# Banded attention as PE blocks with a mask matmul, a two-step scan, and an issue order made by a list scheduler, in place of attention by elementwise products and a four-step chunk scan

## The chip, the cores and the metric

The kernel runs on one core of a Trainium2 chip. Times are device microseconds of one execution. A kernel's time is the median of its runs, and the profile comes from one of those executions; its span is about 2 us shorter than the time of the same run. PE is the matmul engine, PEld its weight load (it overlaps PE), DVE the vector engine, ACT the scalar engine, POOL the GpSimd engine, SP the sync engine that issues most transfers; a "q" behind a name (PEq, SPq) means the engine's instruction sequencer or its transfer queue. PSUM is the memory that matmuls write to; to evict a PSUM tile is to copy it out, after which the tile can be used again.

A run counts as slow when it is over 1.5% above the fastest run of the same kernel. Comparisons use fast runs; where a median over all runs is given, it is called that or all runs were fast.

## The reference, cut to what matters

Two independent halves, concatenated on the last axis. Everything is bf16 in and out; S = 2048, D = 448, 16 heads of 28.

```python
def A(x, wqkv, wo):                      # attention over 8 positions: t, t-2, ..., t-14
    q, k, v = split_heads(x @ wqkv)      # H=16, Dh=28
    idx = pos[:, None] - arange(8)[None] * 2
    logits = einsum("bhsd,bhswd->bhsw", q, k[idx]) * Dh ** -0.5   # masked where idx < 0
    o = einsum("bhsw,bhswd->bhsd", softmax(logits), v[idx])
    return merge_heads(o) @ wo

def B(x, Lambda, Bm, C, log_dt, Dskip):  # complex state of 448, a recurrence over 2048 steps
    dt = exp(log_dt);  Lam_bar = exp(dt * Lambda)
    Bu = x @ (((Lam_bar - 1) / Lambda)[:, None] * Bm).T
    h[t] = Lam_bar * h[t-1] + Bu[t]
    return 2 * real(h @ C.T) + x * Dskip
out = concatenate([A, B], axis=-1)
```

Offsets step by two, so even positions attend to even ones only and odd to odd ones. The change uses that.

## The kernel before

The parts that the change replaces. All of it is straight-line code: the order of the instructions on each engine is the order of the text.

```python
# projections: 192 matmuls, each group of 4 evicted by ACT
def proj(t, dst, joff):
    for j in range(J):
        ps = psum.tile([128, 512], F32, tag="mm")
        for kt in range(4):
            PE.matmul(ps[:, 0:D], xTA[:, kt, j, :], wq[:, kt, t * D:(t + 1) * D], ...)      # L144
        ACT.copy(o_ap, ps[:, 0:D].rearrange("p (h d) -> p d h", h=H))
        next_group()                     # transposes on PE, in between
# ... (halo copies by DMA, parameters, tables)

def ssm_chunk_scan(hf):                  # scan over chunks of T = 4 steps
    # rotate by cos/sin tables ...
    V.tensor_tensor_scan(sc[:, ri, i, :], rT[...], vv[:, ri, i, :], 0.0, ALU.mult, ALU.add)   # L278
    # rotate back ...
# then 72 repair matmuls for the three inner steps (L294-L296), each group evicted by ACT

# attention logits: elementwise products on DVE, then a tree of adds
for g in range(4):
    for wi in range(2):
        V.tensor_tensor(pr..., q_s[:], k_s[:, off:off + J]..., ALU.mult)                      # L327
        V.tensor_tensor(pr[:, 0:14, :], pr[:, 0:14, :], pr[:, 14:28, :], ALU.add)             # L329
        ...
# ... softmax on DVE and ACT
for jg in range(J // JG):
    for w in range(W):
        V.tensor_tensor(pv[:], attn[...].to_broadcast(...), v_s[:, off:off + JG], ALU.mult)   # L380
        for jj in range(JG):
            for kt in range(4):          # an identity matmul that sums over the 8 offsets
                PE.matmul(acc[0:KT, kt, jj, :], pvf[:, jj, KT * kt:KT * (kt + 1)], ident[:], ...)  # L385
    ACT.copy(oT[...], acc[0:KT])
    # ... output projection of the group before
```

Of the kernel before, what the change touches and what calls it, by code (L numbers as in the profile page):

```python
# [9 lines left out]
F32 = mybir.dt.float32  # L10
ALU = mybir.AluOpType
ACTF = mybir.ActivationFunctionType

S, D, H, DH, W = 2048, 448, 16, 28, 8
J = 16
HALO = 14
JK = J + HALO
JH = J * H
KT = 112
T = 4  # L20
NC = S // T
PI = math.pi
SHR = 1.0 - 1e-6
MAGIC = 12582912.0


@with_exitstack
def kernel(
# [17 lines left out]
    V = nc.vector  # L46
    ACT = nc.scalar
    PE = nc.tensor

    const = ctx.enter_context(tc.tile_pool(name="const", bufs=1))  # L50
    psum = ctx.enter_context(tc.tile_pool(name="ps", bufs=4, space=bass.MemoryType.PSUM))
    pst_ctx = ExitStack()
    psum_t = pst_ctx.enter_context(tc.tile_pool(name="pst", bufs=2, space=bass.MemoryType.PSUM))
    ident = const.tile([128, 128], BF16, tag="ident")
    make_identity(nc, ident[:])

    bk = ctx.enter_context(tc.tile_pool(name="b_keep", bufs=1, side="right"))
    bx = ctx.enter_context(tc.tile_pool(name="b_x", bufs=1, side="right"))
    bn_ctx = ExitStack()
    bn = bn_ctx.enter_context(tc.tile_pool(name="b_n", bufs=1, side="right"))  # L60
    ak = ctx.enter_context(tc.tile_pool(name="a_keep", bufs=1))
    qk_ctx = ExitStack()
    qkp = qk_ctx.enter_context(tc.tile_pool(name="a_qk", bufs=1))
    ain_ctx = ExitStack()
    ain = ain_ctx.enter_context(tc.tile_pool(name="a_in", bufs=1))

    def rows112(src):
        return src.rearrange("(k p) n -> p k n", p=KT)
    xnA = ain.tile([128, J, D], BF16, tag="xnA")
    xA_r = A_x[0].rearrange("(p j) d -> p j d", j=J)  # L70
    nc.sync.dma_start(xnA[:, 0:4, :], xA_r[:, 0:4, :])
    nc.sync.dma_start(xnA[:, 4:8, :], xA_r[:, 4:8, :])
    nc.sync.dma_start(xnA[:, 8:12, :], xA_r[:, 8:12, :])
    nc.sync.dma_start(xnA[:, 12:16, :], xA_r[:, 12:16, :])
    wq = ain.tile([KT, 4, 3 * D], BF16, tag="wqkv")
    nc.sync.dma_start(wq[:, 0:2], rows112(A_wqkv)[:, 0:2])
    nc.sync.dma_start(wq[:, 2:4], rows112(A_wqkv)[:, 2:4])

    raws = []
    for i, (vec, name) in enumerate(((B_Lambda_re, "lre"), (B_Lambda_im, "lim"), (B_log_dt, "ld"), (B_Dskip, "dsk"))):  # L80
        raw = const.tile([KT, 4], BF16, tag=name + "_raw", name=name + "_raw")
        nc.sync.dma_start(raw[:], vec.rearrange("(t i) -> i t", i=KT))
        raws.append(raw)
    Cn = bn.tile([KT, 2, 4, D], BF16, tag="Cn")
    nc.sync.dma_start(Cn[:, 0], rows112(B_C_re))
    nc.gpsimd.dma_start(Cn[:, 1], rows112(B_C_im))
    Bn = bn.tile([KT, 2, 4, D], BF16, tag="Bn")
    nc.sync.dma_start(Bn[:, 0], rows112(B_B_re))
    nc.gpsimd.dma_start(Bn[:, 1], rows112(B_B_im))
    xnB = bx.tile([128, 4, T, D], BF16, tag="xnB")  # L90
    xB_r = B_x[0].rearrange("(cb p j) d -> p cb j d", p=128, j=T)
    nc.sync.dma_start(xnB[:, 0:2], xB_r[:, 0:2])
    nc.gpsimd.dma_start(xnB[:, 2:4], xB_r[:, 2:4])

    xTA = ain.tile([KT, 4, J, 128], BF16, tag="xTA")
    CT = bn.tile([KT, 4, 2, D], BF16, tag="CT")
    BT = bk.tile([KT, 4, 2 * D], BF16, tag="BT")
    xT4 = bk.tile([KT, 4, T, NC], BF16, tag="xT4")
    idk = ident[0:KT, 0:KT]

    def g_xta(jg, kt):
        tp = psum_t.tile([128, 4, 128], BF16, tag="tp", name="tp")
        for jj in range(4):
            PE.transpose(tp[0:KT, jj, :], xnA[:, 4 * jg + jj, KT * kt:KT * (kt + 1)], ident[:])  # L104
        V.tensor_copy(xTA[:, kt, 4 * jg:4 * jg + 4, :], tp[0:KT])  # L105

    def g_bt(ri, kt):
        tp = psum_t.tile([128, 4, 128], BF16, tag="tp", name="tp")
        for pt in range(4):
            PE.transpose(tp[0:KT, pt, 0:KT], Bn[:, ri, pt, KT * kt:KT * (kt + 1)], idk)  # L110
        ACT.copy(BT[:, kt, ri * D:(ri + 1) * D].rearrange("p (a b) -> p a b", a=4), tp[0:KT, :, 0:KT])

    def g_x4(kt, j):
        tp = psum_t.tile([128, 4, 128], BF16, tag="tp", name="tp")
        for cb in range(4):
            PE.transpose(tp[0:KT, cb, :], xnB[:, cb, j, KT * kt:KT * (kt + 1)], ident[:])  # L116
        ACT.copy(xT4[:, kt, j, :], tp[0:KT])

    def g_ct(ri, pt):
        tp = psum_t.tile([128, 4, 128], BF16, tag="tp", name="tp")  # L120
        for dtile in range(4):
            PE.transpose(tp[0:KT, dtile, 0:KT], Cn[:, ri, dtile, KT * pt:KT * (pt + 1)], idk)
        V.tensor_copy(CT[:, pt, ri, :].rearrange("p (a b) -> p a b", a=4), tp[0:KT, :, 0:KT])

    groups = ([(g_xta, (jg, kt)) for jg in range(4) for kt in range(4)]
              + [(g_ct, (ri, pt)) for ri in range(2) for pt in range(4)]
              + [(g_bt, (ri, kt)) for ri in range(2) for kt in range(4)]
              + [(g_x4, (kt, j)) for j in range(T) for kt in range(4)])

    def next_group(n=1, late=False):  # L130
        for _ in range(n):
            if groups and (late or groups[0][0] in (g_xta, g_ct)):
                fn, args = groups.pop(0)
                fn(*args)
    next_group(4)

    q_s = qkp.tile([128, DH, J, H], BF16, tag="q_s")
    k_s = qkp.tile([128, JK, DH, H], BF16, tag="k_s")
    v_s = ak.tile([128, JK, DH, H], BF16, tag="v_s")
    def proj(t, dst, joff):  # L140
        for j in range(J):
            ps = psum.tile([128, 512], F32, tag="mm")
            for kt in range(4):
                PE.matmul(ps[:, 0:D], xTA[:, kt, j, :], wq[:, kt, t * D:(t + 1) * D], start=(kt == 0), stop=(kt == 3))  # L144
            o_ap = dst[:, :, j, :] if t == 0 else dst[:, joff + j, :, :]
            ACT.copy(o_ap, ps[:, 0:D].rearrange("p (h d) -> p d h", h=H))  # L146
            next_group()
        if t != 0:
            nc.sync.dma_start(dst[1:65, 0:HALO], dst[0:64, J:JK])
            nc.sync.dma_start(dst[65:113, 0:HALO], dst[64:112, J:JK])  # L150
            nc.sync.dma_start(dst[112:128, 0:HALO], dst[111:127, J:JK])
            nc.sync.dma_start(dst[0:1, 0:HALO], dst[0:1, J:JK])

    proj(2, v_s, HALO)
    def pt_(name):
        return const.tile([KT, 4], F32, tag=name, name=name)
    lre, lim, ld, dsk = [pt_(n) for n in ("lre", "lim", "ld", "dsk")]
    for f_, r_ in zip((lre, lim, ld, dsk), raws):
        V.tensor_copy(f_[:], r_[:])
    hpib = const.tile([KT, 1], F32, tag="hpib")  # L160
    nc.gpsimd.memset(hpib[:], 0.5 * PI * SHR)

    def tt(o, a_, b_, op):
        V.tensor_tensor(o[:], a_[:], b_[:], op)
        return o

    def ts(o, a_, s1, op):
        V.tensor_scalar(o[:], a_[:], s1, None, op)
        return o

    def sincos(sin_out, cos_out, y, kM, pool, shape, tagp):
        nfr = pool.tile(shape, F32, tag=tagp + "nfr", name=tagp + "nfr")
        V.scalar_tensor_tensor(nfr[:], kM, -MAGIC, y, ALU.add, ALU.subtract)
        ACT.activation(sin_out, nfr[:], ACTF.Sin, scale=-2 * PI * SHR)
        afr = pool.tile(shape, F32, tag=tagp + "afr", name=tagp + "afr")
        ACT.activation(afr[:], nfr[:], ACTF.Abs)
        ACT.activation(cos_out, afr[:], ACTF.Sin, bias=hpib[:], scale=-2 * PI * SHR)

    dt = pt_("dt"); ACT.activation(dt[:], ld[:], ACTF.Exp)
    are = tt(pt_("are"), dt, lre, ALU.mult)  # L180
    th = tt(pt_("th"), dt, lim, ALU.mult)
    r = pt_("r"); ACT.activation(r[:], are[:], ACTF.Exp)
    rT = pt_("rT"); ACT.activation(rT[:], are[:], ACTF.Exp, scale=float(T))
    f = ts(pt_("f"), th, 1.0 / (2 * PI), ALU.mult)
    fT = ts(pt_("fT"), th, float(T) / (2 * PI), ALU.mult)
    kM1 = pt_("kM1"); V.tensor_scalar(kM1[:], f[:], 1.0, MAGIC, ALU.mult, ALU.add)
    sn = pt_("sn"); cs = pt_("cs")
    sincos(sn[:], cs[:], f[:], kM1[:], const, [KT, 4], "p_")
    pwall = const.tile([KT, T - 1, 3, 4], F32, tag="pwall")
# [58 lines left out]
    for hf, j in [(hf, j) for hf in range(2) for j in range(T)]:  # L248
        if hf == 0 and j < T - 1:
            next_group(4, late=True)  # L250
# [170 lines left out]
```

## Time and profile before

| | before |
|---|---|
| time, median of 3 runs | 229.51 us (227.4 to 229.69) |
| span of the profiled run | 227.3 us |
| busiest engines | PE 80%, DVE 71% |

The page of the kernel before, parts 1 and 2: busy time with share of the span and number of instructions; then three rows of busy tenths in 40 equal slices of the span (9 is 90% or more), and the row of the clock that PE was granted, in tenths of full speed.

```profile
PE 181.1 (80%) x1400; PEld 118.0 (52%) x1400; DVE 161.9 (71%) x200; ACT 105.1 (46%) x186; POOL 4.8 (2%) x18
...
PE   2008995989997999999969400599999996999993
...
DVE  1103779794007999179999999999867999999022
...
PEclk9999999799999799999999955599999999999999
```

Counting slices from 0, 5.7 us each: PE has one hole in slices 22 to 25 (near 127 to 145 us), with a halved clock in it, and one at the start. The chain that ended last, by engine:

```profile
PE 57%; DVE 25%; ACT 8%; DMA 7%; SPq 1%; issue 1%
```

Busy time by stretch; the columns are the stretch, its length, then busy us and number of instructions of PE, PEld, DVE, ACT and POOL, then the granted PE clock, the busy share of the DMA engines, and GB/s.

```profile
20.00:60.00 40.00, 36.33 (x230) 21.24 (x229) 28.16 (x91) 28.91 (x60) 0.00 (x0) 0.96 0.40 89
60.00:95.00 35.00, 33.43 (x214) 21.06 (x212) 21.92 (x11) 25.37 (x48) 0.11 (x1) 0.95 0.20 36
...
120.00:160.00 40.00, 22.75 (x112) 12.69 (x110) 39.86 (x27) 15.15 (x27) 0.37 (x2) 0.79 0.02 6
160.00:195.00 35.00, 33.05 (x367) 24.18 (x366) 30.74 (x30) 11.71 (x16) 0.47 (x2) 1.00 0.19 59
```

PE is the busier engine from 20 to 95 us and from 160 us on, at 90 to 96% of each stretch. From 120 to 160 us DVE works without a pause and PE 57% of the time. Three of the groups that the change removes, with busy us, mean ns of one, and the idle time just before them:

```profile
L327 DVE TENSOR_TENSOR pr<-q_s,k_s 128x7168 bf16<-128x7168 bf16 x8 | 31.1, 3885 | 15.9 <-ACT q_s L146 15.9
...
L380 DVE TENSOR_TENSOR pv<-attn,v_s 128x1792 bf16<-128x1792 bf16 x32 | 32.2, 1082 | 0.0
L385 PE MATMUL acc<-ident,pv 128*112 128x128 bf16 x512 | 29.2, 219 | 2.0 <-ACT oT L387 2.0
```

### The profile page before, as it was taken

Reading aid. Unit: us, or ns where it says so; the run is one execution under the profiler, and the core shown is the slowest. Engines: PE = TensorE matmul, PEld = TensorE weight load, DVE = VectorE, ACT = ScalarE, POOL = GpSimd, SP = SyncE. Lnnn points to the kernel's source line nnn. Section 1 sums busy time; section 2 is a strip of 40 time slices with the busy share of each in tenths; the row PEclk is TensorE's granted clock in tenths of the full one; section 3 lists DMA queues with packets and bytes.
Section 4 is the critical chain, followed back from the end, with each engine's and each line's share of the span. In section 5 each row is a group of like instructions: output and inputs, shape, how many; then the busy total and the mean of one; then the engine's idle time right before and its main releaser. Section 6 shows DMA issues by size and latency. Waiting matters only on the chain.

```text
span 227.3 us, 3441 instructions
## 1 busy us (share of the span) xinstructions
PE 181.1 (80%) x1400; PEld 118.0 (52%) x1400; DVE 161.9 (71%) x200; ACT 105.1 (46%) x186; POOL 4.8 (2%) x18
## 2 busy tenths in 40 slices
PE   2008995989997999999969400599999996999993
PEld 2004662645555666566536200255555696887961
DVE  1103779794007999179999999999867999999022
ACT  2001691898678876454438300293345213234151
POOL 6000000000000000000000000000000000000000
PEclk9999999799999799999999955599999999999999
DMA  6999300392752000000000000001112230020213
GB/s 227 283 291 204 136 4 0 71 178 40 141 108 35 3 0 0 3 0 0 0 0 0 3 0 0 0 0 40 62 43 81 62 114 3 0 84 3 82 36 128
DMA packets 9996, 14.02 MB, mean 62 GB/s; under 512 B 2716, under 2 KB 8188, under 8 KB 9724
## 3 DMA queue, kind: packets, MB, share of 16 engines
q1 hardware_dynamic: 9612, 12.07, 21.2%
q0 software_dynamic: 368, 1.72, 2.6%
q8 instruction: 11, 0.18, 0.3%
q14 instruction: 5, 0.04, 0.1%
HBM read 6.88 MB, written 3.67 MB: 46 GB/s over the span
## 4 chain that ended last, share of the span: by engine, by line
PE 57%; DVE 25%; ACT 8%; DMA 7%; SPq 1%; issue 1%
PE acc L385 13%; PE ps L144 12%; PE ps L306 11%; DMA wq<-in_A_wqkv_dram 7%; PE psf L256 6%; PE ps L367 5%; DVE pr L327 5%; DVE scr L278 4%; DVE pr L329 3%; DVE dg L212 2%; PE tp L116 2%; PE psf L295 2%; PE psf L296 1%; PE ps L308 1%; PE psf L261 1%; PE psf L260 1%
## 5 line engine op out<-in xcount | busy, mean ns | idle before, releaser
L144 PE MATMUL ps<-wq,xTA 112*128 112x448 bf16 x192 | 44.9, 376 | 15.6 <-DMA wq<-in_A_wqkv_dram 11.9
L327 DVE TENSOR_TENSOR pr<-q_s,k_s 128x7168 bf16<-128x7168 bf16 x8 | 31.1, 3885 | 15.9 <-ACT q_s L146 15.9
L256 PE MATMUL psf<-xT_115,BT 112*112 112x512 bf16 x128 | 33.7, 386 | 0.0
L380 DVE TENSOR_TENSOR pv<-attn,v_s 128x1792 bf16<-128x1792 bf16 x32 | 32.2, 1082 | 0.0
L385 PE MATMUL acc<-ident,pv 128*112 128x128 bf16 x512 | 29.2, 219 | 2.0 <-ACT oT L387 2.0
L385 PEld LDWEIGHTS <-pv 128*112 128x112 bf16 x512 | 29.0, 130 | 2.3 <-issue 2.0
L144 PEld LDWEIGHTS <-xTA 112*128 112x128 bf16 x192 | 18.9, 103 | 20.3 <-issue 4.3
L306 PE MATMUL ps<-Cw,Z 112*128 112x448 bf16 x128 | 26.8, 352 | 0.0
L262 ACT CAST Z<-psf 112x512 bf16<-112x512 f32 x32 | 18.8, 587 | 16.9 <-PE psf L261 15.5
L295 PE MATMUL psf<-Z,dg 112*112 112x511 bf16 x24 | 10.1, 419 | 18.8 <-DVE Z L282 18.8
L297 ACT CAST Z<-psf 112x512 bf16<-112x512 f32 x24 | 14.0, 585 | 22.9 <-PE psf L296 21.7
L256 PEld LDWEIGHTS <-BT 112*112 112x112 bf16 x128 | 16.7, 132 | 9.9
L146 ACT CAST v_s<-ps 128x448 bf16<-128x448 f32 x16 | 8.3, 538 | 26.8 <-PE ps L144 26.7
L105 DVE COPY xTA<-tp 112x512 bf16<-112x512 bf16 x16 | 6.7, 422 | 19.6 <-PE tp L104 19.4
L387 ACT CAST oT<-acc 112x2048 bf16<-112x2048 f32 x4 | 7.5, 1865 | 22.8 <-PE acc L385 22.8
L310 ACT CAST yo<-ps 128x448 bf16<-128x448 f32 x16 | 8.3, 531 | 17.9 <-DMA out_dram<-yo 9.8
L104 PEld LDWEIGHTS <-xnA 128*112 128x112 bf16 x64 | 7.3, 164 | 18.0 <-issue 12.5
L306 PEld LDWEIGHTS <-Z 112*128 112x128 bf16 x128 | 11.8, 98 | 9.0
L329 DVE TENSOR_TENSOR pr<-pr 128x3584 bf16<-128x3584 bf16 x8 | 16.1, 2016 | 0.1
L296 PEld LDWEIGHTS <-dg 112*112 112x112 bf16 x24 | 3.4, 142 | 21.5 <-issue 19.9
L367 PE MATMUL ps<-wo_p,oT 112*128 112x448 bf16 x64 | 12.6, 352 | 0.0
L104 PE MATMUL tp<-ident,xnA 128*112 128x128 bf16 x64 | 7.7, 259 | 4.4 <-DMA xnA<-in_A_x_dram 4.3
(131 smaller groups left out, 234.3 us busy)
## 6 DMA issues: line engine op xcount, KB each, us to landing
xnA<-in_A_x_dram SPq DMA_DIRECT2D x4, 448.0 KB, 6.8
out_dram<-yo SPq DMA_DIRECT2D x16, 112.0 KB, 1.7
out_dram<-ya SPq DMA_DIRECT2D x16, 112.0 KB, 1.7
wq<-in_A_wqkv_dram SPq DMA_DIRECT2D x2, 588.0 KB
xnB<-in_B_x_dram POOLq DMA_DIRECT2D x1, 896.0 KB, 13.2
xnB<-in_B_x_dram SPq DMA_DIRECT2D x1, 896.0 KB
v_s<-v_s SPq DMA_DIRECT2D x1, 784.0 KB
k_s<-k_s SPq DMA_DIRECT2D x1, 784.0 KB
```

Of the source, the lines that this page charges most:

```text
L104: PE.transpose(tp[0:KT, jj, :], xnA[:, 4 * jg + jj, KT * kt:KT * (kt + 1)], ident[:])
L144: PE.matmul(ps[:, 0:D], xTA[:, kt, j, :], wq[:, kt, t * D:(t + 1) * D], start=(kt == 0), stop=(kt == 3))
L256: PE.matmul(ps[:], BT[:, kt, ri * D + KT * pt: ri * D + KT * (pt + 1)], xT4[:, kt, j, :], start=(kt == 0), stop=(kt == 3 and j == 0))
L262: ACT.copy(Z[:, ri * 4 + pt, j, :], ps[:])
L295: PE.matmul(ps[:, 1:NC], dg[:, pt, j, ia, :], Z[:, pt, T - 1, 0:NC - 1], start=False, stop=False)
L297: ACT.copy(Z[:, ri * 4 + pt, j, :], ps[:])
L306: PE.matmul(ps[:, 0:D], Z[:, k8, j, cols], Cw[:, k8, :], start=(k8 == 0), stop=False)
L327: V.tensor_tensor(pr.rearrange("p d (j h) -> p d j h", h=H), q_s[:], k_s[:, off:off + J].rearrange("p j d h -> p d j h"), ALU.mult)
L329: V.tensor_tensor(pr[:, 0:14, :], pr[:, 0:14, :], pr[:, 14:28, :], ALU.add)
L367: PE.matmul(ps[:, 0:D], oT[:, kt, j, :], wo_p[:, kt, :], start=(kt == 0), stop=(kt == 3))
L380: V.tensor_tensor(pv[:], attn[:, w, JG * H * jg:JG * H * (jg + 1)].rearrange("p (j h) -> p j h", h=H) .unsqueeze(2).to_broadcast((128, JG, ...
L385: PE.matmul(acc[0:KT, kt, jj, :], pvf[:, jj, KT * kt:KT * (kt + 1)], ident[:], start=(w == 0 and jj == 0), stop=(w == W - 1 and jj == JG - 1))
```

## The change

The intent: give the attention to PE as small blocks, so that DVE has only the normalising left; halve the work of the state space half by a two-step scan, which runs over the first and then the second half of the positions (the half-scans); let the transfers transpose (the prediction calls such a transfer a crossbar load); and interleave the two halves so that PE never runs dry. The diff replaces nearly the whole body. Its core, cut:

```diff
+# attention: per block of 112 or 128 queries of one parity, 4 mask matmuls and 16 score
+# matmuls in four row groups of 32 (28 used), one exponential, 16 matmuls with V,
+# whose 29th column is ones and gives the sum
+            s4 = h["s4"] = pss.tile([128, 4, 512], F32, tag="s4", name="s4")
+            for g in range(4):
+                PE.matmul(s4[:, g, 0:4 * n]..., msk[32 * g:32 * g + 32, 0, :],
+                          msk[32 * g:32 * g + 32, 1:2, c0:c0 + n].to_broadcast((32, 4, n)), start=True, ...)  # L569
+            for s in range(4):
+                for g in range(4):
+                    PE.matmul(s4[:, g, s * n:s * n + n], Kt[32 * g:32 * g + DH, s, par, k0(b):k0(b) + 128],
+                              Qt[32 * g:32 * g + DH, s, par, q0(b):q0(b) + n], ...)                          # L573
+            ACT.activation(P[...], h["s4"][...], ACTF.Exp, scale=SCALE)                                     # L578
+            for hd in range(H):
+                PE.matmul(av[:, 29 * hd:29 * hd + 29], h["P"][:, hd // 4, hd % 4, :], Vt[:, par, b, hd, :], ...)  # L584
+            V.reciprocal(rc, avv[0:n, :, 28])                                                               # L592
+            V.tensor_tensor(O[...], avv[0:n, :, 0:DH], rc.unsqueeze(2).to_broadcast((n, H, DH)), ALU.mult)  # L593
+# ... x arrives as (t two) d, transposed by the transfer: 7 tiles of 128 x 1024
+        SP.dma_start_transpose(dst[:, :, n * p:n * p + n], src[n * p:n * p + n, :])
+# ... 21 weight scalings, each a product and a multiply-add on DVE
+    def c_set(p, n, dst, m):
+        V.tensor_scalar(tmp[:], CT[:, pm, :], p["p" + n][:, m:m + 1], None, ALU.mult)                       # L455
+        V.scalar_tensor_tensor(dst[:, m, :], CT[:, m, :], p["s" + n][:, m:m + 1], tmp[:], ALU.mult, ALU.add)  # L456
+# ... G = the product of C and B that feeds x of the step itself through: 4 groups of 7 matmuls,
+#     each evicted by DVE
+                PE.matmul(ps[0:n, 0:D], natW[:, m, D + 128 * k:...], C1[:, m, :], ...)                      # L713
+            V.tensor_copy(Gm[0:n, k, :], h["ps"][0:n, 0:D])                                                 # L718
+        n1 = node(f"g{k}", {"P": 1.33}, pe, list(c1.values()), RK_G + 0.1 * k, alloc="mm")
+        gn[k] = node(f"ge{k}", {"V": 0.75}, ev, [n1], RK_G + 0.1 * k, free="mm")
```

The order comes from a scheduler that runs while the kernel is built. Every piece of work is a node with a cost per engine in us, dependencies and a rank. The scheduler plays the engines forward; a free engine takes the ready node of the lowest rank. The instructions are then emitted in order of planned start, and from there on the order on each engine is fixed.

```diff
+RK_V0, RK_Q0, RK_B0, RK_V1, RK_Q1, RK_B1 = 10, 20, 30, 34, 40, 50   # projections, state input
+RK_S0, RK_S1 = 31, 51                                               # first, second half-scan
+RK_C1, RK_C2, RK_G = 45, 47, 52                                     # weight scalings, G
+RK_Y0, RK_Y1, RK_W = 60, 80, 70                                     # outputs
+    plan = Plan({"mm": 3, "s4": 1, "av": 1, "P": 3, ...})           # buffers: three "mm" tiles in PSUM
+    td = node("tdv", {"V": 5.2}, lambda e: tables_dve(prm), [pa], 4)
+    ta = node("tac", {"A": 4.2}, lambda e: tables_act(prm), [td], 4)
+    ...
+    plan.run({"P": 5.3, "A": 4.0, "V": 1.0, "S": 12.0, "G": 15.0})
+    bad = nc.values_load(flag[0:1, 0:1], min_val=0, max_val=128)
+    with tc.If(bad > 0):                                            # a guard: the exact form, if a sum
+        exact_attention(tc, A_x, A_wqkv, A_wo, out)                 # left the range of the fast one
```

## The prediction

> **What bounds the kernel now.** The chain that ended last is 57% PE, 25% DVE, 8% ACT, 7% DMA. The busy table by stretches shows three regimes. From 20 to 95 us and from 160 us on PE is 90 to 95% busy. From 120 to 160 us DVE is busy 39.9 of 40 us and PE only 22.8, at a granted clock of 0.79: DVE multiplies q by k for eight window offsets and the state-space scan waits among that. The first 20 us are a load wait (PE busy 3.7; 11.9 waiting for the qkv weights).
>
> **What goes (groups by busy time).** DVE: logits by multiply and add, about 65 us, softmax 10, attention times v 32.2. PE: 512 identity matmuls that sum over offsets (four blocks of about 7.2 us on the chain), the transposes, the chunk products and repair matmuls (47 us of busy entries), and the hole in the middle. 3 MB of halo copies.
>
> **What comes.** Stream rates in this trace: 0.19 us per 448-column matmul (8 in 1.51 us), 0.2165 per 512-column one (11 in about 2.4). Estimates from them:
> - PE: V 72 x 0.19 = 13.7; q,k 128 x 0.2165 = 27.7; state input 98 x 0.2165 = 21.2; feed-through product 5.3; y 29.2; output projection 64 x 0.19 = 12.2: 109 us. Attention: 18 blocks of 4 mask matmuls, 16 score matmuls in four row groups, 16 of 29 columns. If row groups run together (the Trainium skill, "TensorE: Matmul & The Clock Gate", Part 3, measured 3.07x for four row tiles; no run here shows it yet), 1.1 us a block; if weight loads bind, about 2. I take 1.4: 25 us. Sum 134 us.
> - DVE: a 1024-element bf16 product takes 0.68 us, a 512-long scan 1.20; eight rotate-scan-rotate units about 50 us, normalising about 16, 21 weight scalings at 0.44 + 0.68 about 23.5, padding, tables, parameters about 18: 110 us, and some evacuations.
> - ACT: 18 exponentials of 1792 elements, about 1.65 us each by the 2048-element eviction's 1.87: 30 us; 96 evacuations of 0.53 to 0.59: 54 us, shared with DVE.
> - Tail: a guard flag is read and a branch skips the fallback: 2 to 4 us, a guess.
>
> **Critical path.** PE is the limit nearly throughout. Useful matmuls start at 5 to 6 us (first crossbar loads are 0.46 MB, like the first x loads of before, whose matmul started at 4.3). Then 134 us and about 10% of gaps (one score buffer; a DVE chain from parameters to state weights until about 35 us; the second half-scan must end before the last y tiles): to about 153. Last eviction, output (1.7 us to landing) and branch: 4 to 5. Span about 157; device time 1 to 2 us more, as before (227.3 against 229.5).
>
> **Predicted 158 us, range 144 to 178.** Faster by over 2%: 0.97; within 2%: 0.015; slower: 0.015.
>
> **What would show it.** PE above 85% busy from 10 us on, clock near 1; DVE 75 to 85%; no 15-us PE hole; the chain at least 60% PE; attention blocks of 1.1 to 1.4 us on PE; scan units about 50 us of DVE; useful matmuls from about 6 us.
>
> **What would make it wrong.** Row groups that do not overlap (+15 us of PE). Crossbar loads slower than plain ones, starving the first 30 us, or state-weight transposes queued behind each other. DVE as the real limit: its in-order stream of scan, normalisation and evacuations pushing the second half-scan to 140 us and leaving PE cold. A costly or taken fallback branch. In the good direction: fewer gaps, 145 us.

## The result, and the profile after

| | before | after |
|---|---|---|
| time, median of 4 runs | 229.6 us (227.4 to 230.9) | 177.79 us (177.64 to 178.79) |
| span | 227.3 us | 176.1 us |
| ratio of fast runs | | 0.7778 (95%: 0.7713 to 0.7842) |

A ratio is the mean time of one kernel's fast runs over the mean of the other's fast runs of the same rounds, so it is not quite the ratio of the two medians. The result passed the comparison and the guard did not take the fallback. The change saves 52 us where 71.5 were predicted, and 177.8 lies at the upper edge of the predicted range: the direction was right, the size was not.

The page after, with the rows as before:

```profile
PE 140.0 (79%) x1221; PEld 70.2 (40%) x1231; DVE 117.7 (67%) x259; ACT 85.9 (49%) x116; POOL 24.9 (14%) x53
...
PE   7969913997999999799789942302999999999970
...
DVE  0769966699799999999999999999540037200000
...
PEclk9999996599999999999999995555699999999998
```

Two holes in the PE row, with 4.4 us to a slice: one in slices 5 and 6 (22 to 29 us), one in slices 23 to 27 (101 to 122 us). The clock falls to 5 or 6 in slices 6 and 7, and in 24 to 28. In the chain that ended last DVE now comes first:

```profile
DVE 44%; PE 37%; POOL 9%; ACT 4%; issue 3%; DVEq 0%; POOLq 0%; ACTq 0%
```

The stretches, cut at the holes:

```profile
0.00:20.00 20.00, 17.05 (x69) 7.28 (x71) 12.97 (x33) 8.12 (x17) 17.67 (x39) 1.00 1.00 230
20.00:40.00 20.00, 13.32 (x67) 5.47 (x67) 15.47 (x55) 10.15 (x13) 5.82 (x12) 0.83 0.15 32
40.00:100.00 60.00, 55.05 (x572) 27.59 (x579) 56.95 (x108) 40.13 (x51) 1.40 (x3) 1.00 0.45 86
100.00:122.00 22.00, 6.11 (x140) 3.73 (x136) 21.20 (x38) 6.65 (x4) 0.00 (x0) 0.64 0.03 6
122.00:176.00 54.00, 48.46 (x384) 26.13 (x383) 11.08 (x28) 20.87 (x33) 0.00 (x0) 0.94 0.29 85
```

From 100 to 122 us PE is busy for 6.11 of 22 us and DVE for 21.20. After 122 us it is the reverse: 48.46 of 54 us of PE, and DVE has little left. The two engines work one after the other here. Busy time flatters PE, too: part of it is at a low clock.

The waits; the columns are who waited, for whom, us in total, how often, and the longest:

```profile
PE mm L713 <- DVE Gm L719: 8.8, 1, 8.8
PE mm L543 <- DVE Qt L475: 6.6, 1, 6.6
...
PE s L569 <- ACT P L578: 5.5, 3, 1.8
...
PE av L584 <- DVE O L593: 3.5, 5, 1.3
```

The two long waits are one wait each. The later one, in PE's and DVE's lists in order of time (start us, duration us, engine, line, operation, count, and in brackets the idle time before it and what ended it). PE first, then DVE:

```profile
104.57 0.37 PE L569 MATMUL s<-msk 32*128 32x448 bf16 x4
104.77 0.37 PE L573 MATMUL s<-Qt,Kt 28*128 28x112 bf16 x16
106.97 0.56 PE L569 MATMUL s<-msk 32*128 32x448 bf16 x4 [1.83 <-ACT P L578]
...
112.81 0.60 PE L573 MATMUL s<-Qt,Kt 28*128 28x112 bf16 x16
122.24 2.77 PE L713 MATMUL mm<-C,natW 128*64 128x448 bf16 x7 [8.82 <-DVE Gm L719]
124.94 2.52 PE L779 MATMUL mm<-wo,OT 128*128 128x448 bf16 x8
```

```profile
119.49 0.42 DVE L676 TENSOR_TENSOR ra<-rs,tab 128x512 bf16<-128x512 bf16 x1
...
120.73 0.42 DVE L679 TENSOR_TENSOR h<-ra 64x512 bf16<-64x512 bf16 x1
121.16 0.63 DVE L718 CAST Gm<-mm 128x448 bf16<-128x448 f32 x1
121.89 0.29 DVE L719 TENSOR_TENSOR Gm<-mm,dgE 128x128 bf16<-128x128 f32 x1
```

This is how the two lists are read together. The fourth group of the feed-through product G needs a PSUM tile. The three tiles of that pool hold its first three groups, whose evictions stand on DVE behind the last instruction of the second half-scan (L679). They start the moment that the scan ends, at 121.16 us, and PE goes on when the first tile is free. Behind the waiting matmul stands the output projection (L779), which needs a tile of the same pool and runs straight after it. The outputs of the first half (y, L754) take all of G as input, so they wait as well. Before the hole, from 102 to 113 us, PE had only attention blocks left to run, three of which waited 1.8 us each for the exponential that frees the one score buffer.

The earlier hole, in PE's and DVE's lists:

```profile
29.14 9.71 PE L543 MATMUL mm<-xA,Wpad 128*128 128x512 bf16 x31 [6.62 <-DVE Qt L475]
38.78 0.39 PE L569 MATMUL s<-msk 32*128 32x512 bf16 x4
39.01 0.39 PE L573 MATMUL s<-Qt,Kt 28*128 28x128 bf16 x16
```

```profile
27.26 1.23 DVE L407 TENSOR_SCALAR tmpB<-tmpB 128x2048 int32<-128x2048 int32 x1 [2.16 <-ACT tab L406]
28.40 0.68 DVE L475 CAST Qt<-mm 128x512 bf16<-128x512 f32 x1
```

DVE makes twelve instructions of table work, waits 2.16 us for ACT's sine, takes the absolute value that ACT's cosine needs, and only then evicts a PSUM tile of q; PE had stood since 22.5 us. The 31 matmuls after the hole took 9.71 us, against 6.7 at the stream rate of 0.2165 us. The Trainium skill ("TensorE: Matmul & The Clock Gate", Part 1) states that the PE clock halves after an idle window of about 3.4 us. The first hole agrees: after 6.62 us of standing still the clock is at half, and it is full again at about 34.5 us, 5.4 us after the matmuls resume. The later hole does not fit so simply. The clock was at half before that hole began at 113.4 us: at 106.97 us the four mask matmuls took 0.56 us, where they had taken 0.37 at 104.57, and since 100 us PE had not stood still for longer than 1.83 us at a time.

### Where the 176.1 us go

A sum from the numbers of the trace. The first useful matmul starts at 7.2 us and the last one ends at 170.7, so the tail takes 5.4. In the 163.5 us between them there are 109.3 us of projection, state and output matmuls at the stream rates named in the prediction, and 18 attention blocks. A block of 112 queries takes about 0.95 us of PE: 0.20 from the start of its masks to that of its scores, 0.30 for the scores, 0.45 for the product with V. That makes 17.1 us, so 126.4 us of work in all and **37 us of gaps and slow clock, where 13 were predicted**. Of these, 6.6 are the first hole and 3.0 the slow matmuls after it. 17.5 lie between 100 and 122 us, where only about 4.5 us of work at full rate were done (8.8 of them are the wait for G). The other 10 are smaller waits and about 2 us of slow matmuls just after 122 us.

### The profile page after: what moved, and what is told of

Same layout as the page of the kernel before. It is cut to its first block, busy times and chain, and to the rows that moved or that the text cites. A ratio compares the mean times of both kernels' runs of the same rounds, so it can differ in the third digit from the quotient of the medians.

```text
span 176.1 us, 3132 instructions
## 1 busy us (share of the span) xinstructions
PE 140.0 (79%) x1221; PEld 70.2 (40%) x1231; DVE 117.7 (67%) x259; ACT 85.9 (49%) x116; POOL 24.9 (14%) x53
## 4 chain that ended last, share of the span: by engine, by line
DVE 44%; PE 37%; POOL 9%; ACT 4%; issue 3%; DVEq 0%; POOLq 0%; ACTq 0%
PE mm L754 12%; DVE rs L658 9%; PE mm L779 7%; PE mm L543 5%; DVE C L456 4%; PE mm L757 3%; DVE wtmp L455 3%; DVE O L593 3%; PE mm L623 3%; DVE ra L669 2%; PE av L584 2%; DVE rb L645 2%; DVE rb L670 2%; DVE ra L644 2%; POOL mst L293 2%
## 5 line engine op out<-in xcount | busy, mean ns | idle before, releaser
L543 PE MATMUL mm<-xA,Wpad 128*128 128x512 bf16 x122 | 31.0, 405 | 6.9 <-DVE Qt L475 6.6
L578 ACT ACTIVATE P<-s 128x1792 bf16<-128x1792 f32 (+1 forms) x18 | 30.4, 1687 | 9.5 <-PE s L573 9.4
L473 ACT CAST ys<-mm 128x448 bf16<-128x448 f32 x30 | 16.0, 532 | 37.5 <-PE mm L779 17.3
L754 PE MATMUL mm<-C,h 128*128 128x448 bf16 x112 | 23.8, 352 | 0.0
L623 PE MATMUL mm<-xB,WT 128*128 128x512 bf16 x94 | 21.8, 379 | 0.2
L543 PEld LDWEIGHTS <-Wpad 128*128 128x128 bf16 x128 | 12.7, 103 | 23.1 <-issue 10.4
L592 DVE RECIPROCAL rcs<-av 112x16 f32<-112x16 f32 (+1 forms) x18 | 4.5, 250 | 17.5 <-PE av L584 17.5
L526 PE MATMUL mm<-Wv,xA 128*128 128x448 bf16 x72 | 14.8, 353 | 0.5 <-ACT Vt L473 0.5
L754 PEld LDWEIGHTS <-h 128*128 128x128 bf16 x112 | 10.5, 98 | 8.6
L779 PE MATMUL mm<-wo,OT 128*128 128x448 bf16 x64 | 13.8, 368 | 0.0
L593 DVE TENSOR_TENSOR O<-av,rcs 112x448 bf16<-112x448 f32 (+1 forms) x18 | 11.2, 624 | 0.6
```

The source lines that it names most:

```text
L473: ACT.copy(o, i)
L526: PE.matmul(ps[:, 0:D], xA[:, 3 * par + k, k0(b):k0(b) + 128], Wv[:, 4 * par + k, :], start=(k == 0), stop=(k == 3))
L543: PE.matmul(ps[:], Wpad[:, 4 * par + k, q, 128 * s:128 * s + 128], xA[:, 3 * par + k, 512 * c:512 * c + 512], start=(k == 0), stop=(k == 3))
L578: ACT.activation(P[:].rearrange("p s g q -> p g s q")[:, :, :, 0:n], h["s4"][:, :, 0:4 * n].rearrange("p g (s q) -> p g s q", s=4), ACTF.E ...
L593: V.tensor_tensor(O[0:n, D * par:D * par + D].rearrange("p (h d) -> p h d", h=H), avv[0:n, :, 0:DH], rc.unsqueeze(2).to_broadcast((n, H, D ...
L623: PE.matmul(ps[:], WT[:, k, 128 * m:128 * m + 128], xB[:, k, HALF * hf:HALF * hf + HALF], start=(k == 0), stop=(k == 6))
```

## The experiments

Four theories, named by letters in the expectations; a number behind a letter means the same theory about a later version.

- **O, the order.** The order fixed by the ranks makes PE wait: G before the second half-scan's end, and the start with its tables. Mending ranks and costs brings most of the 24 us back, with the same work.
- **D.** DVE's sum of work is the limit: it is over 95% busy from 40 to 121 us. Taking work off it shortens the kernel by about as much.
- **P.** PE's sum of work is the limit after all. Taking matmuls away shortens the kernel by as much.
- For the mended kernel, **B** (both sums together bind, so that only both cuts show) and **F** (the fixed order absorbs a cut, and it only shows when the scheduler is told of it).

The runs: e1 to e4 (chip 2), e5 to e8 (chip 4), e9 to e12 (chip 10), e13 to e16 (chip 5), and e17 with e18 (chip 5 again). The kernel before had medians of 230.7 to 232.4 us there. Comparisons across calls lean on the ratios to it. In the call of e13 to e16 only 3 of its 11 runs were fast, and the record calls the verdicts of e13 and e16 unclear, so within that call times are compared. Costs and ranks are literals, so several experiments change only the order of the same instructions.

### e1_dve_cut: 14 DVE instructions fewer

Gives a wrong result: the second term of the C scalings is dropped. (It still passed the comparison's tolerance, as did all kernels below that are wrong, so a pass is weak evidence.)

```diff
 def c_set(p, n, dst, m):
-    V.tensor_scalar(tmp[:], CT[:, pm, :], p["p" + n][:, m:m + 1], None, ALU.mult)
-    V.scalar_tensor_tensor(dst[:, m, :], CT[:, m, :], p["s" + n][:, m:m + 1], tmp[:], ALU.mult, ALU.add)
+    V.tensor_scalar(dst[:, m, :], CT[:, m, :], p["s" + n][:, m:m + 1], None, ALU.mult)
```

> Wrong result on purpose: the 14 weight scalings on DVE between 74 and 95 us lose their first product and become one instruction each, in the same order. Theory D (DVE's in-order stream is the limit from 10 to 122 us, and PE's last 49 us start only when it ends): about 12 us less DVE work before the second half-scan, so about 12 us faster than the change, 166 us. Theory P (PE is the limit nearly throughout, as predicted): under 3 us, 175 to 178.

Measured: 174.98 us, ratio 0.7556 (0.7492 to 0.7619). DVE's busy time fell by 11.3 us (117.7 to 106.4), the time by 3 (by 5 if the ratios are compared). DVE waits instead: its reciprocals waited 21.6 us for the attention product, against 17.5. The wait of PE in front of G's fourth group is still 7.6 us. D in its strong form falls.

### e2_pe_cut: a quarter of the q/k matmuls fewer

Also wrong.

```diff
-    for k in range(4):
+    nk = 4 if c == 0 else 2
+    for k in range(nk):
         PE.matmul(ps[:], Wpad[...], xA[:, 3 * par + k, 512 * c:512 * c + 512], start=(k == 0), stop=(k == nk - 1))
```

> Wrong result on purpose: the 16 projections of q and k of the second token half (62 to 82 us) sum over 2 instead of 4 matmuls, 32 matmuls of 0.2165 us less on PE, 6.9 us. Theory D: under 1.5 us gained, 176 to 178. Theory P: 6 to 7 us gained, 171.

Measured: 177.83 us, ratio 0.7681 (0.7622 to 0.7741), with 32 matmuls or 6.9 us of PE work less: 0 to 2 us. PE's busy time did fall, by 5.1 us (140.0 to 134.9); other waits of PE grew, such as that for the normalising before a product with V (3.5 to 6.2). P falls. The prediction had called PE the limit nearly throughout.

### e3_g_early: one number

```diff
-RK_C1, RK_C2, RK_G = 45, 47, 52
+RK_C1, RK_C2, RK_G = 45, 47, 47.8
```

> One constant: the rank of the feed-through product (four PSUM tiles and their DVE evictions) goes from after the second half-scan to before it. No work is added or taken away. Theory O (PE stands still from 113 to 122 us and runs at 6 of 20 us from 100 to 120 because three PSUM tiles wait for DVE evictions behind the scan, and the first half of y waits with them): y of the first half moves into that hole, 10 to 14 us faster than the change, 164 to 168. If DVE's total alone decides (everything on PE after 122 us needs the second half-scan), no gain. Theory P: no gain.

Measured: 164.7 us, ratio 0.7117 (0.7063 to 0.717). Same work, another rank for G, 13 us less (15 by the ratios). The evictions of G now stand before the second half-scan (94.7 to 99.2 us). The stretch that held the hole:

```profile
100.00:122.00 22.00, 22.00 (x219) 11.77 (x218) 21.29 (x36) 12.39 (x15) 0.00 (x0) 1.00 0.14 39
```

PE is busy for all 22 us at full clock, where it was 6.11 at 0.64. The output matmuls of the first half now run while DVE does the second half-scan. O is confirmed for this hole.

### e4_calibrated: only the costs told to the scheduler

The durations that the profile after shows were put in for the literals: for example the parameters 3.1 for 1.6, the tables 7.0 for 5.2 on DVE and 5.7 for 4.2 on ACT, a weight scaling 1.21 for 0.98. Ranks as in the change.

```diff
-    td = node("tdv", {"V": 5.2}, lambda e: tables_dve(prm), [pa], 4)
+    td = node("tdv", {"V": 7.0}, lambda e: tables_dve(prm), [pa], 4)
 # ... a dozen more costs likewise
```

> The scheduler's DVE and ACT costs set to the durations of the trace (tables 7.0 instead of 5.2 us, odd v weights 3.8 instead of 1.0, weight scalings 1.21 instead of 0.98 and so on); no other edit. Theory C (the order is bad because its costs are too low): the q evictions leave DVE's queue behind the tables, the 6.6-us hole at 22 us shrinks, 4 to 8 us faster, 170 to 174. Rivals D and O: under 2 us, since the DVE sum and the rank of the feed-through product stay.

Measured: 180.62 us over all runs, two of four slow; fast ones 179.64 and 178.37, ratio 0.7732 (0.765 to 0.7814). The same as the change. In the profiled run, which is one of the slow ones, the first hole shrank from 6.6 to 3.4 us, and the second grew by more:

```profile
PE mm L713 <- DVE Gm L719: 15.6, 1, 15.6
```

A gain at the start was given back in front of the scan's end. This is the same hole as before, so costs alone did not mend it. (e11 below shows the same long wait in a fast run.)

### e5_abs_act: the absolute values on ACT (with G early)

```diff
-    V.tensor_scalar(ang.bitcast(I32), ang.bitcast(I32), 0x7FFFFFFF, None, ALU.bitwise_and)
+    ACT.activation(ang, ang, ACTF.Abs)
 # and the small one (af) likewise
```

> On top of the early feed-through rank (164.7 us): the two absolute values between the two sine passes move from DVE to ACT, nothing else. Theory T (PE's 6.6-us hole at 22 us: q evictions stand in DVE's queue behind the absolute value, which waits for ACT's first sine): they can start when the tables' DVE part ends at 24.9 instead of 28.4, so the hole shrinks by about 3 us and the kernel gains 2 to 3.5 us, 161 to 163. Rival (the hole is hidden later, since DVE is the limit from 40 us on whatever PE does before): DVE work before 37 us falls by only 1.2 us, gain about 1 us.

Measured: 160.72 us, ratio 0.6928 (0.6865 to 0.6991): 4 us under e3. The first hole fell from 6.6 to 3.5 us. The tables no longer pass from DVE to ACT to DVE to ACT.

### e6_tmp_act: 21 products moved from DVE to ACT (with G early)

```diff
-    V.tensor_scalar(tmp[:], CT[:, pm, :], p["p" + n][:, m:m + 1], None, ALU.mult)
+    ACT.activation(tmp[:], CT[:, pm, :], ACTF.Identity, scale=p["p" + n][:, m:m + 1])   # bf16, 2 buffers
```

> On top of the early feed-through rank: the first product of all 21 weight scalings moves from DVE to ACT (with its temporary in bf16), 9.4 us less DVE work, about 11 us more ACT work. Theory D2 (with the order mended DVE's stream up to about 137 us is the limit): 5 to 9 us faster, 156 to 160. Rival B (PE and DVE are balanced, as the DVE cut of the unmended order gave only 3 of 12 us): at most 3 us faster.

Measured: 168.48 us, ratio 0.7268 (0.7204 to 0.7332): 4 us slower than e3. Both expectations missed. The product takes about 0.68 us on ACT against 0.45 on DVE, and the scheduler was not told: its plan still had it as DVE's. DVE waited:

```profile
DVE natW L450 <- ACT wtmp L449: 7.7, 7, 3.1
DVE C L456 <- ACT wtmp L455: 7.0, 6, 2.2
```

Moving work to a less busy engine cost time here: it put a hand-over into each of 21 steps, and DVE waited at 13 of them. Whether a plan with the true cost would have gained, no run shows.

### e7_prologue and e8_prologue_cal: the start mended, without and with measured costs

e7 is e5 with the four parameter rows loaded first, on ACT's queue, and the two V-weight copies on ACT. e8 is e7 with the measured costs of e4.

```diff
+    for i, vec in enumerate((B_Lambda_re, B_Lambda_im, B_log_dt, B_Dskip)):
+        ACT.dma_start(rows[7 * i:7 * i + 7, :], vec.rearrange("(c p) -> c p", p=64))
-        V.tensor_copy(Wv[64:128, 4:8, :], Wv[0:64, 0:4, :])     # and the second one
+        ACT.copy(Wv[64:128, 4:8, :], Wv[0:64, 0:4, :])
-    vo = node("vwo", {"V": 1.0}, lambda e: vw_odd(), [], 0, at=6.0)
+    vo = node("vwo", {"A": 3.4}, lambda e: vw_odd(), [], 0, at=6.0)
```

> On top of the early feed-through rank: the four parameter rows are loaded first on ACT's queue instead of through the software queue, the odd v weights are copied by ACT, the absolute values by ACT. The parameter chain can start at about 4 instead of 10.3 us and the scheduler then puts the tables before the weight padding. Theory S (the 12 us by which the start runs behind its plan are passed on to the end): the first state weight is scaled at 24 to 27 us instead of 37, and 5 to 9 us are gained, 156 to 160. Rival: q starts later (20 instead of 15.6 us), gain under 2 us.

e7 measured: 165.45 us over all runs, fast ones 165.1 and 163.06, ratio 0.7079 (0.6978 to 0.718). No gain over e5; it is slower. Against e3 it is 0.5 (fast runs) to 1 us (ratios) faster, as the rival said, and q did start later, at 21.6 us. The first state weight was scaled at 29 us, not at 24 to 27. The start had changed under a plan with the old costs, and e8 changes only these.

> The same three moves with the scheduler's costs set to the durations of the trace, which puts the padding before the tables. Theory S: smaller gain, the first state weight at 31 to 33 us, 158 to 162. If measured costs by themselves give a better order, it beats the run before it; the calibrated costs alone had made the change slower by 1 to 3 us.

e8 measured: 153.36 and 152.97 us in its fast runs, 156.44 and 156.51 in two others that count as slow; the ratio of the fast ones, worked out from these runs, is 0.661 (no interval was given). The stretches that held the two holes:

```profile
20.00:40.00 20.00, 18.12 (x152) 8.55 (x152) 18.68 (x62) 18.73 (x23) 1.32 (x3) 1.00 0.33 60
...
100.00:122.00 22.00, 22.00 (x208) 12.10 (x206) 21.32 (x36) 11.45 (x19) 0.00 (x0) 1.00 0.19 64
```

Both are closed: 18.12 us of PE against 13.32 in the first one. It is faster than S expected. Why its runs fall into two groups was not found out; the six runs of e16, the same kernel, spread from 153.4 to 157.5 us without clear groups.

### e9_cal_g: measured costs and G early, nothing else

```diff
-RK_C1, RK_C2, RK_G = 45, 47, 52
+RK_C1, RK_C2, RK_G = 45, 47, 47.8
 # and the costs of e4
```

> Only the order differs from the change: early feed-through rank (alone 164.7 us) plus the measured costs (alone 180.6 us, slower than the change). No instruction is moved to another engine. Theory O2 (the costs only lost because the late feed-through product turned every gain of the start into a longer hole before it): with the hole mended they now gain, 157 to 161 us. Rival (measured costs just give a worse order): 164 us or more.

Measured: 160.31 us, ratio 0.6944 (0.6893 to 0.6995). The costs that were worth nothing in e4 are worth 4 us when G is early. With e4 and e3 this makes a square: costs alone nothing, rank alone 13 us, both 17.5 (by the ratios, 0.7732, 0.7117 and 0.6944 against 0.7778, it is 1, 15 and 19).

### e10_order_best: e8 without moving the parameter rows

```diff
-    tr = node("tr", {"P": 0.2}, lambda e: tr_rows(), [], 0, alloc="mm", at=4.0)
+    tr = node("tr", {"P": 0.2}, lambda e: tr_rows(), [], 0, alloc="mm", at=9.8)
 # rows again on POOL's queue, as in the change
```

> The candidate without the rows' move: early feed-through rank, measured costs, absolute values and odd v weights on ACT, the parameter rows expected at 9.8 us where the trace has them. The best run so far (154.9 us median, fast runs 153) also loads the rows first, which delays the v weights to 8.96 us. If the rows' move is worth nothing, this gives 151 to 155 us; if an early parameter chain matters, 155 to 160.

Measured: 155.5 us, ratio 0.6724 (0.6674 to 0.6774). This lies on the border of the two expectations: 2.4 us above the fast runs of e8 and 1.1 above those of e16, both on other chips. Loading the rows first is worth no more than that. e9, without the absolute values and copies on ACT, took 160.31 us, so these moves are worth about 5 us.

### e11_no_g: e8 with G late again

```diff
-RK_C1, RK_C2, RK_G = 45, 47, 47.8
+RK_C1, RK_C2, RK_G = 45, 47, 52
```

> The best run so far with the feed-through rank put back to where the change had it, after the second half-scan. Theory O (that rank decides whether earlier gains reach the end): PE's hole before the feed-through product comes back at 12 to 18 us, 167 to 175 us. Rival (the start was the main cause, the rank matters little once it is mended): under 160 us.

Measured: 175.36 us, ratio 0.7614 (0.7546 to 0.7681): 20 us above e10 and 22 above the fast runs of e8, and the wait in front of G's fourth group is back:

```profile
PE mm L713 <- DVE Gm L719: 15.7, 1, 15.7
```

With G late, nearly everything that was won at the start is lost in front of the scan's end. This is the same experiment as e3, done from the other side, and it settles O for the second hole.

### e12_pe_cut_mended, e13_dve_cut_mended, e14_both_cut_mended: the cuts again, on e8

e8 runs near the predicted 158 us. Is it now bound by a sum of work? e12 is e8 with the edit of e2, e13 with that of e1, e14 with both.

> Wrong result on purpose: the cut of 32 matmuls, 6.9 us of PE, that gave nothing on the change itself, now on the best run so far. Theory P2 (with the order mended PE is the limit, as the prediction had it): 4 to 7 us faster, 147 to 150 us. Rival (DVE still is): under 2 us.

e12 measured: 157.04 us over all runs, two slow; fast ones 156.47 and 154.74, ratio 0.6735 (0.6659 to 0.6812). No gain from 6.9 us of PE work less: e10 took 155.5 us, the fast runs of e8 and e16 153 to 155.

> Wrong result on purpose: the DVE cut (14 weight scalings become one instruction each, about 12 us) on the mended order. Theory D3 (DVE's stream decides when the feed-through product and the second half-scan end, and PE's last 50 us hang on it): 7 to 12 us faster than the mended order, 143 to 148 us. Rival B (balance): at most 4 us faster.

e13 measured: 152.79 us, ratio 0.6651 (0.6552 to 0.675). One of its four runs, the profiled one, counts as slow; the fast ones average 152.2 us, against 154.5 for the fast runs of e16. About 2 us from 12 us of DVE work less (its busy time is 102.9 us, in e8 114.9).

> Wrong result on purpose: both cuts, 12 us of DVE and 6.9 us of PE, on the mended order. Theory D3: the same as with the DVE cut alone within 1.5 us. Rival B: clearly more than either alone, 6 us or more beyond the DVE cut.

e14 measured: fast runs 151.3 and 150.89, two slow ones at 154; ratio of the fast ones, worked out, 0.660. The fast ones are 3.4 us under those of e16 and 1.1 under those of e13. So with this order neither sum binds, nor both together: P, D and B all fall for the mended kernel as it is ordered. Its PE list shows what stands still; a matmul group of the second half's state input behind an attention product that waits for the normalising of the block before:

```profile
67.81 1.68 PE L621 MATMUL mm<-xB,WT 128*128 128x512 bf16 x7
71.38 0.55 PE L582 MATMUL av<-Vt,P 128*128 128x29 bf16 x16 [1.89 <-DVE O L591]
71.78 2.59 PE L621 MATMUL mm<-xB,WT 128*128 128x512 bf16 x7
```

### e15_bf16_tmp: a cheaper product (on e8)

```diff
-    tmp = wk.tile([128, D], F32, tag="wtmp", name="wtmp", bufs=1)
+    tmp = wk.tile([128, D], BF16, tag="wtmp", name="wtmp", bufs=1)
```

> Correct kernel: the temporary of the 21 weight scalings is bf16 instead of f32, so its product should take about 0.28 instead of 0.45 us, 3.5 us of DVE in all. Theory D3: 2 to 3.5 us faster than the mended order. Rival B: within 1 us.

Measured: 153.49 us over all runs, fast ones 153.25 and 151.09. The product fell from 0.45 to 0.33 us, not to 0.28, and DVE's busy time by 2.7 us. The time fell by 1.3 (medians) to 2.3 us (fast runs) against e16, within the spread of that kernel's own runs. It does not decide between D3 and B.

### e16_mended_again: e8 once more, in five rounds

The same kernel as e8, to have a firm number on this chip.

> The mended order again (three moves, measured costs, early feed-through rank), unchanged, more rounds: 153 to 157 us, to know how far its two groups of runs lie apart and to have it on the chip of the cuts.

Measured: 154.83 us (153.37 to 157.48, one of six slow), ratio 0.6752 (0.6689 to 0.6815).

### e17_both_cut_replanned: e14, with the cuts told to the scheduler

The same instructions as e14; only three cost literals differ (q and k of the second half, and both sets of C scalings), and with them the order.

```diff
-    n1 = node(f"q{q}{par}{s}{c}", {"P": 0.865}, pe, wp, r, ...)
+    n1 = node(f"q{q}{par}{s}{c}", {"P": 0.865 if c == 0 else 0.433}, pe, wp, r, ...)
-    c1[m] = node(f"c1{m}", {"V": 1.21}, ..., RK_C1 + 0.1 * m)        # c2 likewise
+    c1[m] = node(f"c1{m}", {"V": 0.33}, ..., RK_C1 + 0.1 * m)
```

> Wrong result on purpose: the same two cuts (12 us of DVE, 6.9 us of PE) as the run that gained 2 us, but the scheduler is told the smaller costs and orders anew. Theory F (the fixed order absorbed the cuts): 5 to 10 us faster than that run, 143 to 148 us. Rival R (a third resource, such as ACT's exponentials or the transposes of the outputs): under 2 us, 150 to 153.

Measured: 145.62 us, ratio 0.6307 (0.6264 to 0.635): fast runs against fast runs 5.6 us less than e14, with the same instructions. That is what F expected: in e14 the fixed order absorbed part of the cuts. The stretch from 40 to 100 us, first in e14, then in e17, where DVE is busy again:

```profile
40.00:100.00 60.00, 53.38 (x579) 27.38 (x578) 47.41 (x100) 38.08 (x48) 1.40 (x3) 0.97 0.43 79
```

```profile
40.00:100.00 60.00, 57.62 (x627) 30.18 (x626) 56.07 (x116) 39.18 (x53) 1.40 (x3) 1.00 0.48 86
```

Two things stay untested: which of the two cuts brings the gain, and whether this order would also be better for the uncut kernel. The kernel is wrong, so 145.6 us is no result, only a sign of where the gain had gone.

### e18_nm_bf16: a correct try with what was learnt

e8 with the bf16 product, its cost told (1.04), and the normalising given an early rank, so that attention products wait less.

```diff
-    n4 = node(f"n{par}{b}", {"V": 0.83}, nm, [n3], r, ...)
+    n4 = node(f"n{par}{b}", {"V": 0.83}, nm, [n3], 5 + 0.1 * i, ...)
-    c1[m] = node(f"c1{m}", {"V": 1.21}, ..., RK_C1 + 0.1 * m)        # c2 and lam likewise
+    c1[m] = node(f"c1{m}", {"V": 1.04}, ..., RK_C1 + 0.1 * m)
```

> Correct kernel, on the mended order: the normalisation of an attention block comes before everything else in DVE's order as soon as it is ready, so that PE's next block isn't held up behind the scan, and the temporaries of the weight scalings are bf16 (0.33 instead of 0.45 us each), both known to the scheduler. Theory F: 1.5 to 4 us faster than the mended order (154.8 us), 150.5 to 153. Rival R: 153 to 155.5.

Measured: 154.06 us, ratio 0.6684 (0.6637 to 0.673). By 0.4% (fast runs) to 1% (ratios) under e16, which is the rival's range; the intervals overlap. F's expectation was missed. Its six runs lie within 152.86 to 154.8, and it beats both kernels of the change: 154 us against 178 and 230. e8, e15 and e18 cannot be told apart safely.

## Why the prediction was wrong

Point by point:

- **The mechanism was right.** The attention left DVE, the identity matmuls and the repair matmuls went, and the two halves overlap. How the 52 us that the change saves divide among these, no run separates.
- **The work sums held.** PE: 134 us predicted, 126 worked out from the trace. An attention block takes 0.95 us of PE, where I took 1.4 and expected 1.1 to 1.4. DVE: 110 us "and some evacuations" predicted, 117.7 measured, with about 50 us for the scan units as predicted. The four row groups do overlap (see the last section).
- **Start and tail were nearly right.** 7.2 us against 5 to 6, where the first useful matmul runs straight after 14 warm-up matmuls, with no wait before it; 5.4 against 4 to 5. No branch was taken.
- **The step that failed is the term "about 10% of gaps", 13 us, and the claim under it, "PE is the limit nearly throughout".** The gaps and the slow clock measured 37 us. The errors of the terms in us: start +2, work -8, gaps +24, tail +1, together 19 of the 20 that the prediction missed by; the rest is the distance of span and time. By luck, the work that was put too high hid 8 us of the gaps. The predicted marks failed with it: PE above 85% from 10 us on (it is 80%, and 28% from 100 to 122 us), DVE 75 to 85% (67%), clock near 1 (0.92 on average), the chain at least 60% PE (37%), no long PE hole (two).
- **What stands in its place.** PE's queue is in order, and so is DVE's. The Trainium skill ("TensorE: Matmul & The Clock Gate", Part 1, its note on queue depths) states this for DVE and ACT, and that PE only pulls weight loads ahead. The trace agrees: DVE stood for 2.16 us at the absolute value (27.26 us) with evictions of q behind it whose matmuls had ended by 22.5. PE stood for 1.32 us at a product with V (74.26 us) with mask matmuls behind it (74.75) that use a constant mask and a score buffer which ACT had freed at 67.7. I had read the scan's end as something that the last output tiles wait for. In fact all four evictions of G waited for it, by one rank: 52 against the scan's 51, and with them G's fourth group and the outputs of the first half. Changing that number alone gave 13 us (e3), and undoing it in the mended kernel cost 20 to 22 (e11). This could have been seen without a run. The plan that the kernel computes while it is built (a model, not a measurement) has PE standing from 97.1 to 103.3 us in front of G's fourth group, and with the rank of e3 it ends 12.1 us sooner (139.6 instead of 151.7).
- **The start.** I had seen "a DVE chain from parameters to state weights until about 35 us" and put it into the 10%. The same plan puts the first weight scaling at 25.4 us; the trace has it at 37.1. Its costs were too low: 5.2 for tables that take 7.0, 1.6 for parameters that take 3.1. Mending costs and hand-overs at the start gave about 10 us on top of e3 (164.7 to the 153 to 155 of e8 and e16).
- **One of my own warnings was the right one**, "its in-order stream of scan, normalisation and evacuations pushing the second half-scan ... and leaving PE cold", but as a limit of DVE's sum. e1 shows that it was not the sum: 11 us of DVE work less gave 3 to 5.
- **With the order mended the kernel takes 153 to 155 us**, close to the 158 predicted. That is no proof that the prediction's reasons were right: e12 to e14 show that neither PE's sum nor DVE's limits even that kernel as it is ordered, and e17 that another order of the same instructions is faster.

Open: which hand-over limits e18, as no single wait of PE in it is longer than 1.9 us; why the runs of e8 and e16 spread by over 2%; and how far a better order could go, because e17 shows only, on a cut kernel, that a better order exists, not what the best one is.

## What to carry to other kernels

When the order on each engine is fixed in advance, sum the work of each engine for a lower bound, but then look for the instruction whose buffer is freed by an engine that has something long in front of it: that wait blocks everything behind it on its own engine too. Read the plan's own idle stretches before predicting. If a cut of work gives nothing, make the order anew with the true costs before concluding that the work did not matter. A scheduler's ranks and costs are part of the kernel's performance: here one rank was worth 13 us, and true costs were worth nothing until that rank was right.

## What the Trainium skill lacked or had wrong

- "TensorE: Matmul & The Clock Gate", Part 3, gives 3.07 times for four row tiles of 32 rows with 512 columns. Here the four mask matmuls of 448 columns passed in 0.20 us from their start to the start of the scores, and one alone takes 0.19, so 4 x 0.19 / 0.20, about 3.8 times. But the 16 score matmuls with 112 columns, each with its own weights, took 0.30 us where 16 x 112 columns at the same rate would take 0.76: 2.5 times. Taken together the 20 matmuls took 0.50 us where 1.52 would be needed one after the other: 3.0 times, near the page's figure. How the gain divides between masks and scores is uncertain, since the profile only models the ends of matmuls. Whether the width or the changing weights make a difference, no run here separates. The lines behind this:

```profile
54.86 0.37 PE L569 MATMUL s<-msk 32*128 32x448 bf16 x4
55.06 0.37 PE L573 MATMUL s<-Qt,Kt 28*128 28x112 bf16 x16
55.36 2.44 PE L526 MATMUL mm<-Wv,xA 128*128 128x448 bf16 x12
```

- "Perfetto Trace Analysis", section "Identifying the Most-Contended Engine", says to take the engine with the highest occupancy (for the matmul engine it asks for other measures) and "Optimize this engine first." The page also tells to look for the gaps of that engine and for what ends them, which is how e3 was found here. It lacks the warning that in a statically ordered kernel this may show nothing: DVE was 95% busy from 40 to 121 us and PE 92% from 40 to 100, yet cutting 12 and 6.9 us of their work gave 0 to 5 us (e1, e2, e12 to e14), until the order was made anew (e17: fast runs 145.5 against 151.1 of e14).
- "DMA: Bandwidth & Descriptors", section "DMA Transpose (X-bar)", tells which engines may issue a transpose, but not how long a large one from HBM holds the queue that issues it. Two of 0.46 MB held the sync engine's queue for 4.71 us here, the plain load of 0.34 MB behind them for 0.59 us and the next one for 2.22, so six plain loads stood behind two transposes.
- "TensorE: Matmul & The Clock Gate", Part 1, does not give how little work within a window still counts as idle. Here the clock went to half at about 106.2 us, after a stretch (102 to 106 us) in which PE was busy for 1.31 of 4 us, with no wait longer than 1.83 us.
